# First sequence's frequency product in plain float32, its threshold subtraction on GpSimd, and another form of the MLP weights' conversion

## The chip, the cores and the metric

The kernel runs on one core of one Trainium2 chip. The metric is device time of one execution in microseconds (us), here the median of three: 1941.88 us (1940.3 to 1946.44). A core has TensorE (PE, matrix products), VectorE (DVE), ScalarE (ACT) and GpSimd (POOL), each with its own instruction queue that is worked off in order, and SyncE (SP), which here issues every DMA.

## The reference

Eight sequences of 3136 positions with 256 channels go through a frequency-domain layer and then through a block with an MLP:

```python
X = np.fft.rfft(x, axis=1)
Xr, Xi = (X.real.astype(np.float32), X.imag.astype(np.float32))
Yr = Xr @ w_r - Xi @ w_i + b_r
Yi = Xr @ w_i + Xi @ w_r + b_i
lam = 0.01
Yr = np.sign(Yr) * np.maximum(np.abs(Yr) - lam, 0.0)
Yi = np.sign(Yi) * np.maximum(np.abs(Yi) - lam, 0.0)
x = np.fft.irfft(Yr + 1j * Yi, n=x.shape[1], axis=1)
...
X = np.fft.fft(x, axis=1)
X = np.fft.fft(X, axis=2)
u = x + np.real(X).astype(np.float32)
un = (u - mean(u)) / np.sqrt(var(u) + 1e-06)
out = u + np.maximum(un @ w_ch1, 0.0) @ w_ch2
```

w_r and w_i are 256x256 in float32. The MLP weights w_ch1 (256x1024) and w_ch2 (1024x256) arrive in float64.

## The kernel before

**Split products.** Most products take operands in two parts, a high part rounded to the type float32r and a low part with the rest, also float32r. `mm3` (lines 152 to 155) then issues three matmuls: high x low, low x high, high x high. The high part is written by a copy on ACT, the low part by a subtraction, `lo_v` on VectorE (L147) or `lo_g` on GpSimd (L150).

**Stages.** The transform over 3136 = 64 x 49 positions is done in two steps by matrix products. Stage one (`p1`) makes the 64-point transforms of a sequence and stores them in DRAM (`ad`; `a0` for the first eight rows of sequence 0). `p2_f2` loads them (`af`, L415, with a table `tff`, L417) and makes the 49-point step (L431), in four quarters q of a sequence with four parts `ui` each; its result is the spectrum X of the quarter, 2 halves of 128 channels x 8 rows x (real, imaginary) x 50. `p2_w` multiplies by the complex weight, adds the bias and applies the threshold. `p2_mix` makes the channel transform of the second block's FFT2 and stores it to `md`; `p2_yt` transposes the thresholded spectrum Y (L621), `p2_g2` applies the inverse 49-point step (L648) and stores to `bd`. Then, for a pair of sequences, `p3_norm` loads `bd` (`bf`) and `md` (`mt`), makes the inverse 64-point step, adds and normalizes; `p3_tr` transposes (L731), `p3_mlp1` and `p3_mlp2` are the MLP (tiles h and o). So the MLP needs the whole of sequence 0 before it starts, and the MLP of earlier sequences hides the front stages of later ones.

**Sequence 0** has nothing to hide behind. All its stages are in plain float32 with one matmul each (`fwd_0`, `KF["cs"]`, `tif`, `yf`), except the frequency product, which uses `mm3` as for the other sequences.

**The frequency product** (L479 to 500). The complex product takes three real ones: with the sum Xs = Xr + Xi, `ks` = w_r·Xs, real part `ks` + ws·Xi, imaginary part `ks` + wd·Xr, where ws = -w_i - w_r and wd = w_i - w_r are made on VectorE at the start (L220) and split. For each quarter, each half o of the output channels and each of the three products, `prod` runs over the two halves k of the contraction. So there are 2 x 3 products of 400 columns a quarter and 24 in a sequence, each of two `mm3` (six matmuls); the prediction calls the two contraction halves of one product a pair. After the second and third, VectorE makes y = product + bias + ks (L493) and the clamp m of y to ±0.01 (L495), and Y = y - m is the threshold (L496). For sequence 0, VectorE does all of L496; for the others VectorE does half o = 0 and GpSimd o = 1. In the first quarter GpSimd also clears two elements of Y (L500 MEMSET); the transposes L621 read Y after that.

**The operands of the product** (L446 to 461). ACT copies X from PSUM to `xx`, rounds it to `Xh`, GpSimd makes `Xl`; VectorE makes the sum `xs` (L453), ACT rounds it to `Xsh`, GpSimd makes `Xsl`. For ui of 2 and 3 of sequence 0 the operands come from PSUM directly (L456 to 459): the sum is L458, and `Xl` is made on VectorE (L147). Odd quarters of sequence 0 keep the four parts in the buffers (tags) `uth`, `utl`, `bh`, `bl`, even ones in `Xh`, `Xl`, `Xsh`, `Xsl`.

**The MLP weights** (`weights`, `split_double`). They arrive as pairs of 32-bit words and are turned on the chip into high and low float32r parts, in eight tiles of 128 x 512 values. Two raw tiles of 128 x 512 words each are loaded (tags `hh`, `bf`), one tile ahead. For each half of 256 values ACT takes the absolute value of the high word (L171), VectorE keeps its sign and one exponent bit (L177) and shifts the low word (L184). On the full 512, VectorE clips (L172), shifts (L174), xors (L178), extracts the exponent (L181) and scales the low word (L186); ACT rounds the high part (L190), GpSimd subtracts it (L192) and adds the scaled low word (L193).

**What sets the order.** Each stage is a generator that yields due times; the program takes the stage with the smallest (heap at L806 to 815), with 10000 units for a sequence, a quarter of sequence 0 every 0.13 of that, and the conversion's tile j at 1.14 + 0.065 j. The framework then orders each engine's instructions by its own simulated schedule and works out the semaphores; on the chip each engine runs its list in order. `behind(key, ...)` (L262) makes a load wait in the order for the issue of an `af` load. Tiles of one tag share its buffers: a new tile waits for the last reader of the one that it replaces. In PSUM the tag `g` has four buffers for all stages up to the transposes L731.

The core of the product and the subtraction:

```python
mm3(gw, K[name][0][:, k, os_], K[name][1][:, k, os_], *r, start=k == 0, stop=k == 1)
...
va.scalar_tensor_tensor(y1, gw, bias[:, c, o:o + 1], ks, op0=ALU.add, op1=ALU.add)
m = sb.tile([128, 8, S], F32, tag="m", bufs=1, name="m")
va.tensor_scalar(m, y1, -LAM, LAM, op0=ALU.max, op1=ALU.min)
(va if b == 0 or o == 0 else gp).tensor_sub(y[:, o, :, c, :], y1, m)
```

Of the kernel before, what the change touches and what calls it, by code (L numbers as in the profile page):

```python
# [131 lines left out]
def spectral_block(ctx: ExitStack, tc: tile.TileContext, x, w_ri, b_ri, w1, w2,  # L132
# [28 lines left out]
    def split_double(name, h, l, sl, src):  # L161

        def tmp(tag, bufs, dt=I32):
            return sb.tile([128, 512], dt, tag=tag, bufs=bufs, name=f"cv_{name}_{tag}")

        halves = [(t[:, 0::2], t[:, 1::2], np.s_[:, 256 * e:256 * e + 256]) for e, t in enumerate(src)]
        tf = tmp("mt", 2, F32)
        for lo, hi, at in halves:  # L170
# [1 line left out]
        va.tensor_scalar(tf, tf, HI_MIN, HI_MAX, op0=ALU.max, op1=ALU.min)  # L172
# [3 lines left out]
        for lo, hi, at in halves:  # L176
            va.tensor_scalar(w[at], hi, -0x80000000, 0x40000000, op0=ALU.bitwise_and, op1=ALU.bitwise_or)  # L177
# [4 lines left out]
        r = tmp("mt", 2)  # L182
        for lo, hi, at in halves:
            va.tensor_scalar(r[at], lo, 8, None, op0=ALU.logical_shift_right)  # L184
# [1 line left out]
        va.scalar_tensor_tensor(rf, r, 2.0 ** -44, e.bitcast(F32), op0=ALU.mult, op1=ALU.mult)  # L186
# [22 lines left out]
    def load_consts():  # L209
# [191 lines left out]

    def p2_f2(b):


        for q in range(4):
# [57 lines left out]
    def p2_w(b):  # L463

        for q in range(4):
# [7 lines left out]
            def prod(name, o, x_, c=None):  # L473
                g = gtile("g_w")
                gw = g[:, :400].rearrange("p (a j) -> p a j", j=S)
                os_ = slice(o * 128, o * 128 + 128)
                for k in range(2):
                    r = [z[0][:, k] if len(z) == 1 else z[k] for z in x_]
                    if c is not None:  # L479
                        r = [z[:, :, c] for z in r]  # L480
                    mm3(gw, K[name][0][:, k, os_], K[name][1][:, k, os_], *r, start=k == 0, stop=k == 1)
                return gw

            for o in range(2):
# [4 lines left out]
                for c in range(2):
                    yield base + STEP * WW * (o / 2 + (c + 1) / 6)  # L490
                    gw = prod(("ws", "wd")[c], o, xs_[:2], 1 - c)
# [4 lines left out]
                    (va if b == 0 or o == 0 else gp).tensor_sub(y[:, o, :, c, :], y1, m)  # L496
# [356 lines left out]
```

## Time and profile before

| | before |
|---|---|
| median of three runs | 1941.88 us (1940.3 to 1946.44) |
| the profiled execution: span | 1937.1 us |
| instructions | 34781 |
| bytes moved by DMA | 233.03 MB, mean 120 GB/s |
| mean time of an o matmul (256 columns, L154) | 285 ns x1568 |
| mean time of an h matmul (L153) | 389 ns x832 |
| L751 on VectorE (low part of the MLP's middle layer) | 272.2 us x416 |

The span is that of the profiled execution on the core, from its first record to its last; the runs' times lie some 5 us above it, since they hold what is around it. The page gives busy time for each engine, the same in 40 slices of the span, DMA queues, the chain of work that ended last (followed back from the last instruction to what released it), and groups of instructions by line, engine and operation. In a group's row "out<-in" are the tiles written and read, "x" the count; behind the bar stand the busy time, the mean of one in ns, and the idle time just before them with what ended it. In rows of single records the first number is the start, the second the length, both in us, and square brackets hold a wait and what ended it. Tables of waits give "waiting engine, tile, line <- releaser: us, count, mean".

### The profile page before, as it was taken

The numbers are of one execution on the slowest core, as the hardware profiler recorded it, in microseconds if no ns is written. First come the engines' busy times: TensorE is split into PE (matmuls) and PEld (weight loads), VectorE is DVE, ScalarE is ACT, GpSimd is POOL, SyncE is SP. The second block draws the span as 40 slices with busy tenths as digits, with TensorE's granted clock in tenths as the row PEclk, the third lists the DMA queues.
The fourth block names the chain that finished last, engine by engine and source line by source line (L and its number), as shares of the span: only waits on it lengthen the run. The fifth ranks groups of instructions, "written<-read, shape, count | busy, mean of one in ns | idle before, by whom it ended". The sixth has DMA issues, their size and how long they took to land.

```text
span 1937.1 us, 34781 instructions
## 1 busy us (share of the span) xinstructions
PE 1841.4 (95%) x12115; PEld 1692.0 (87%) x12115; DVE 1320.5 (68%) x2847; ACT 850.6 (44%) x1896; POOL 707.5 (37%) x1087
## 2 busy tenths in 40 slices
PE   4785999999999999999999999999999999999999
PEld 2564899989999999989999999998999999998999
DVE  3974777767777667767667677766777776675543
ACT  2454545445444445444444545444544443433322
POOL 1544444344444334344333444324443332322110
PEclk7997999999999999999999999999999999999999
DMA  8766544355343545335453544435533333223210
GB/s 222 188 180 184 151 128 126 95 146 148 105 112 114 151 124 137 98 102 149 117 137 98 152 129 115 129 95 144 148 94 110 98 105 99 68 79 105 65 40 25
DMA packets 164178, 233.03 MB, mean 120 GB/s; under 512 B 27612, under 2 KB 107556, under 8 KB 164004
## 3 DMA queue, kind: packets, MB, share of 16 engines
q1 hardware_dynamic: 164004, 230.82, 42.9%
q8 instruction: 96, 1.57, 0.3%
q14 instruction: 78, 0.64, 0.1%
HBM read 127.95 MB, written 102.76 MB: 119 GB/s over the span
## 4 chain that ended last, share of the span: by engine, by line
PE 75%; DVE 5%; DMA 4%; SPq 3%; issue 1%; POOL 1%; ACT 1%; DVEq 0%; POOLq 0%; ACTq 0%
PE o L154 8%; PE o L153 8%; PE o L155 8%; PE h L153 8%; PE h L154 8%; PE h L155 8%; PE g_f L431 4%; PE g_w L153 3%; PE g_w L155 3%; PE g_w L154 3%; PE g_g L153 2%; PE g_g L154 2%; PE g_g L155 2%; PE g_ut L731 2%; PE g_yt L621 2%; DMA md<-mq 1%
## 5 line engine op out<-in xcount | busy, mean ns | idle before, releaser
L154 PE MATMUL o<-w2h,hl 128*128 128x256 f32 x1568 | 431.5, 285 | 10.9 <-DVE hl L751 10.9
L751 DVE SCALAR_TENSOR_TENSOR hl<-h,hh 128x512 fp32r<-128x512 f32 (+1 forms) x416 | 272.2, 655 | 239.8 <-ACT hh L750 238.6
L750 ACT ACTIVATE hh<-h 128x512 fp32r<-128x512 f32 (+1 forms) x416 | 238.0, 573 | 440.8 <-PE h L155 385.1
L155 PE MATMUL o<-w2h,hh 128*128 128x256 f32 x1568 | 423.9, 280 | 0.0
L153 PE MATMUL o<-w2l,hh 128*128 128x256 f32 x1568 | 397.3, 286 | 3.6 <-DVE ut L770 2.6
L153 PE MATMUL h<-utl,w1h 128*128 128x512 f32 (+1 forms) x832 | 323.5, 389 | 7.0 <-DVE hl L751 7.0
L154 PE MATMUL h<-uth,w1l 128*128 128x512 f32 (+1 forms) x832 | 318.0, 382 | 0.0
L155 PE MATMUL h<-uth,w1h 128*128 128x512 f32 (+1 forms) x832 | 316.7, 381 | 0.0
L154 PEld LDWEIGHTS o<-w2h,hl 128*128 128x128 f32 x1568 | 296.3, 189 | 18.0 <-DVE hl L751 13.6
L153 PEld LDWEIGHTS o<-w2l,hh 128*128 128x128 f32 x1568 | 285.4, 189 | 16.8 <-ACT Xsh L440 2.9
L155 PEld LDWEIGHTS o<-w2h,hh 128*128 128x128 f32 x1568 | 296.4, 189 | 3.1
L150 POOL TENSOR_TENSOR bl<-bf,bh 128x512 fp32r<-128x512 f32 x104 | 130.1, 1252 | 307.0 <-ACT bh L690 302.3
L155 PEld LDWEIGHTS h<-uth,w1h 128*128 128x128 f32 x832 | 156.8, 188 | 24.1
L153 PEld LDWEIGHTS h<-utl,w1h 128*128 128x128 f32 x832 | 157.1, 189 | 21.9 <-DVE hl L751 7.9
L431 PEld LDWEIGHTS g_f<-tff,af 98*128 98x128 f32 x1024 | 142.8, 197 | 36.3 <-issue 22.6
L431 PE MATMUL g_f<-tff,af 98*128 98x100 f32 x1024 | 149.8, 276 | 25.5 <-DMA af<-ad 12.3
L150 POOL TENSOR_TENSOR xl<-xf,xh 128x512 fp32r<-128x512 f32 (+1 forms) x75 | 98.2, 1310 | 203.2 <-ACT xh L374 197.1
L154 PEld LDWEIGHTS h<-uth,w1l 128*128 128x128 f32 x832 | 157.0, 189 | 13.0
L150 POOL TENSOR_TENSOR Xl<-xx,Xh 128x400 fp32r<-128x400 f32 (+1 forms) x96 | 107.5, 1122 | 77.0 <-ACT Xh L440 72.1
L695 DVE TENSOR_TENSOR ut<-g_g,mt 128x512 f32<-128x512 f32 x104 | 68.3, 656 | 97.2 <-PE g_g L155 72.4
L150 POOL TENSOR_TENSOR Xsl<-xs,Xsh 128x200 fp32r<-128x200 f32 x120 | 78.4, 654 | 149.3 <-ACT Xsh L440 140.6
L713 DVE TENSOR_SCALAR nm<-ut,ag,rs 128x256 f32<-128x256 f32 x196 | 88.3, 490 | 48.9 <-POOL rs L710 48.6
(155 smaller groups left out, 3790.1 us busy)
## 6 DMA issues: line engine op xcount, KB each, us to landing
bd<-bev SPq DMA_DIRECT2D x128, 196.0 KB
af<-ad SPq DMA_DIRECT2D x62, 392.0 KB
bf<-bd SPq DMA_DIRECT2D x184, 128.0 KB
out_dram<-ut SPq DMA_DIRECT2D x92, 256.0 KB
xf<-in_x SPq DMA_DIRECT2D x176, 128.0 KB
ad<-ev SPq DMA_DIRECT2D x168, 128.0 KB
md<-mq SPq DMA_DIRECT2D x112, 192.0 KB
mt<-md SPq DMA_DIRECT2D x416, 32.0 KB
```

What stands on the lines that cost most here:

```text
L150: gp.tensor_sub(out_, full, hi.bitcast(F32))
L153: te.matmul(o, lh, rl, start=start, stop=False)
L154: te.matmul(o, ll, rh, start=False, stop=False)
L155: return te.matmul(o, lh, rh, start=False, stop=stop)
L431: te.matmul(g[:, o:o + 100], afs[s][:, ui * D + k * 128:ui * D + k * 128 + 128], tfs[s][:, ui], start=True, stop=True)
L621: te.transpose(gt[:100, (v * 2 + o) * 128:(v * 2 + o + 1) * 128], y[:, o, place].rearrange("p c j -> p (c j)"), ident)
L695: va.tensor_add(ut[:, :n], g[:, :w].rearrange("p (n d) -> p n d", d=D), mt[:, :n])
L713: va.tensor_scalar(nm[:, j], ut[:, j], ag[:, j, 0:1], rs[:, j], op0=ALU.subtract, op1=ALU.mult)
L731: te.transpose(gv[:, k, j * 128:(j + 1) * 128], nm[:, j, k * 128:(k + 1) * 128], ident)
L750: sc.activation(hh[:, :w], h[:, :w], AF.Relu)
L751: va.scalar_tensor_tensor(hl[:, :w], h[:, :w], 0.0, hh[:, :w].bitcast(F32), op0=ALU.max, op1=ALU.subtract)
```

## The change

**The product.** For sequence 0 `x_tiles` now gives two plain float32 tiles, X and Xs. `p2_f2` makes them with an ACT copy from PSUM and one addition on GpSimd; `xx`, `im`, `xs` and the high and low parts are gone for that sequence. `prod` issues one plain float32 matmul for each contraction half in place of `mm3`. The unsplit w_r and ws stay in a tile with the tag `Xl` (`wrsf`), wd in one with the tag `Xsl`, for as long as sequence 0 needs them; before, they were in `hh` and `hl`.

**The threshold.** For sequence 0 all 16 subtractions Y = y - m of 128 x 400 go to GpSimd.

**The conversion.** One raw tile of 128 x 1024 words (tag `utl`, one DMA of 512 KB) takes the place of two of 128 x 512. ACT's absolute value and VectorE's and/or (L177, now L176) work on 512 values at once in place of twice 256. The clip (L172) moves to GpSimd. The shift of the low word (L184) is gone: L186 (now L182) reads the word as unsigned and multiplies by 2^-52 in place of 2^-44.

```diff
@@ split_double
-        halves = [(t[:, 0::2], t[:, 1::2], np.s_[:, 256 * e:256 * e + 256]) for e, t in enumerate(src)]
+        lo, hi = src[:, 0::2], src[:, 1::2]
         tf = tmp("mt", 2, F32)
-        for lo, hi, at in halves:
-            sc.activation(tf[at], hi.bitcast(F32), AF.Abs)
-        va.tensor_scalar(tf, tf, HI_MIN, HI_MAX, op0=ALU.max, op1=ALU.min)
+        sc.activation(tf, hi.bitcast(F32), AF.Abs)
+        gp.tensor_scalar(tf, tf, HI_MIN, HI_MAX, op0=ALU.max, op1=ALU.min)
...
-        for lo, hi, at in halves:
-            va.tensor_scalar(w[at], hi, -0x80000000, 0x40000000, op0=ALU.bitwise_and, op1=ALU.bitwise_or)
+        va.tensor_scalar(w, hi, -0x80000000, 0x40000000, op0=ALU.bitwise_and, op1=ALU.bitwise_or)
...
-        r = tmp("mt", 2)
-        for lo, hi, at in halves:
-            va.tensor_scalar(r[at], lo, 8, None, op0=ALU.logical_shift_right)
...
-        va.scalar_tensor_tensor(rf, r, 2.0 ** -44, e.bitcast(F32), op0=ALU.mult, op1=ALU.mult)
+        va.scalar_tensor_tensor(rf, lo.bitcast(U32), 2.0 ** -52, e.bitcast(F32), op0=ALU.mult, op1=ALU.mult)
@@ load_consts
-        for name, tag in (("wr", "hh"), ("ws", "hh"), ("wd", "hl")):
-            KF[name] = sb.tile([128, 2, D], F32, tag=tag, bufs=2, name=name + "f")
+        keep = sb.tile([128, 2, 2, D], F32, tag="Xl", bufs=1, name="wrsf")
+        KF["wr"], KF["ws"] = keep[:, 0], keep[:, 1]
+        KF["wd"] = sb.tile([128, 2, D], F32, tag="Xsl", bufs=1, name="wdf")
@@ x_tiles
-        if b == 0 and q % 2:
-            return [[sb.tile([128, 8] + c + [S], F32R, tag=t + z, bufs=2, name="X" + z) for k in range(2)]
-                    for t, c in (("ut", [2]), ("b", [])) for z in "hl"]
+        if b == 0:
+            if q % 2:
+                return [[sb.tile([128, 8] + c + [S], F32, tag=t + "h", bufs=2, name="X0") for k in range(2)]
+                        for t, c in (("ut", [2]), ("b", []))]
+            return [[sb.tile([128, 2, 8] + c + [S], F32, tag=t + "h", bufs=1, name="X0")]
+                    for t, c in (("X", [2]), ("Xs", []))]
@@ p2_f2
+                if b == 0:
+                    X, Xs = xq
+                    put(sc.copy, [X], gv)
+                    for x_, s_ in zip(X, Xs):
...
+                        gp.tensor_add(s_, c0, c1)
+                    continue
...
-                if ui < (3 if b else 2):
+                if ui < 3:
@@ p2_w
+                    if b == 0:
+                        te.matmul(gw, KF[name][:, k, os_], r[0], start=k == 0, stop=k == 1)
+                        continue
                     mm3(gw, K[name][0][:, k, os_], K[name][1][:, k, os_], *r, start=k == 0, stop=k == 1)
...
-                    (va if b == 0 or o == 0 else gp).tensor_sub(y[:, o, :, c, :], y1, m)
+                    (gp if b == 0 or o else va).tensor_sub(y[:, o, :, c, :], y1, m)
@@ weights
-            for e, tag in enumerate(("hh", "bf")):
-                t = sb.tile([128, 512], I32, tag=tag, bufs=2, name="raw_" + name)
-                behind(1, out=t, in_=srcs[e])
+            raw[j] = t = sb.tile([128, 1024], I32, tag="utl", bufs=2, name="raw_" + name)
+            v = t if name == "w1" else t.rearrange("p (f e) -> p f e", f=2)
+            behind(1, out=v, in_=src)
```

The change also moves instructions in the engines' lists, up to about the stage where sequence 0 ends; behind that the lists agree. Three places follow. A row is the line, the operation, the tile written and read, and the shape; "x2" stands for two such in a row.

On SP's queue, the loads around those of the second and third raw weight tile (`raw_w`), before:

```order
L266 DMA raw_w_321<-in_w 128x512
L266 DMA raw_w_323<-in_w 128x512
L417 DMA tff<-c_tf 98x400
L415 DMA af<-ad_79 98x1024 x2
L266 DMA xf<-in_x 64x512 x4
L266 DMA raw_w_424<-in_w 128x512
L266 DMA raw_w_426<-in_w 128x512
L415 DMA af<-ad_79 98x1024
L266 DMA tif<-c_ti 100x392 x2
```

and after:

```order
L263 DMA raw_w_284<-in_w 128x1024
L263 DMA tif<-c_ti 100x392
L417 DMA tff<-c_tf 98x400
L263 DMA tif<-c_ti 100x392
L415 DMA af<-ad_79 98x1024 x2
L263 DMA xf<-in_x 64x512 x4
L415 DMA af<-ad_79 98x1024
L263 DMA raw_w_352<-in_w 128x1024
L263 DMA raw_w_447<-in_w 128x1024
```

The third raw tile (raw_w_424 and raw_w_426 before, raw_w_352 after) is now issued behind the third of these `af` loads and behind both `tif` loads.

On VectorE's queue, from the conversion of that third tile on, before:

```order
L177 TENSOR_SCALAR cv_w_ut<-raw_w_424 128x256
L184 TENSOR_SCALAR cv_w_mt<-raw_w_424 128x256
L177 TENSOR_SCALAR cv_w_ut<-raw_w_426 128x256
L184 TENSOR_SCALAR cv_w_mt<-raw_w_426 128x256
L172 TENSOR_SCALAR cv_w_mt<-cv_w_mt 128x512
L174 TENSOR_SCALAR cv_w_mt<-cv_w_mt 128x512
L493 SCALAR_TENSOR_TENSOR y_369<-g_w,bias,ks 128x400
L178 TENSOR_TENSOR cv_w_ut<-cv_w_ut,cv_w_mt 128x512
L495 TENSOR_SCALAR m<-y_369 128x400
```

and after (L505 is the former L493, L507 the former L495):

```order
L176 TENSOR_SCALAR cv_w_ut<-raw_w_352 128x512
L505 SCALAR_TENSOR_TENSOR y_313<-g_w,bias,ks 128x400
L507 TENSOR_SCALAR m<-y_313 128x400
L174 TENSOR_SCALAR cv_w_mt<-cv_w_mt 128x512
L177 TENSOR_TENSOR cv_w_ut<-cv_w_ut,cv_w_mt 128x512
L505 SCALAR_TENSOR_TENSOR y_339<-g_w,bias,ks 128x400
L180 TENSOR_SCALAR cv_w_ut<-cv_w_ut 128x512
```

The first sum y of the product stands behind one operation on that raw tile in place of six.

On GpSimd's queue, between the two MEMSETs of Y in the first quarter, before:

```order
L500 MEMSET Y 128x2
L150 TENSOR_TENSOR Xl<-xs,Xh 128x100 x2
L192 TENSOR_TENSOR cv_w_ut<-cv_w_ut,w1h 128x512
L150 TENSOR_TENSOR Xl<-xs,Xh 128x100 x2
L193 TENSOR_TENSOR w1l<-cv_w_ut 128x512
L150 TENSOR_TENSOR Xl<-xx,Xh 128x2x200
L500 MEMSET Y 128x2
```

and after, with the third tile's clip ahead of them (L172 clip, L452 sum Xs, L508 subtraction Y = y - m, L512 the MEMSETs, L188 and L189 the weights' subtraction and addition):

```order
L172 TENSOR_SCALAR cv_w_mt<-cv_w_mt 128x512
L452 TENSOR_TENSOR X_263<-X_261 128x100
...
L512 MEMSET Y 128x2
L452 TENSOR_TENSOR X_264<-X_262 128x100
L508 TENSOR_TENSOR Y<-y_387,m 128x8x50
L452 TENSOR_TENSOR X_421<-X_420 128x2x100
L189 TENSOR_TENSOR w1l<-cv_w_ut 128x512
L188 TENSOR_TENSOR cv_w_ut<-cv_w_ut,w2h 128x512
L508 TENSOR_TENSOR Y<-y_404,m 128x8x50
L172 TENSOR_SCALAR cv_w_mt<-cv_w_mt 128x512 x2
L189 TENSOR_TENSOR w2l<-cv_w_ut 128x512
L512 MEMSET Y 128x2
```

Low parts `Xl` have left this stretch; sums, subtractions and clips have come. The second MEMSET now stands behind all four subtractions of the first quarter and behind five clips, counted from the one shown first.

More of the change, by code (lines that the diff above doesn't have):

```diff
@@ L13 @@
 I32 = mybir.dt.int32
+U32 = mybir.dt.uint32
 AF = mybir.ActivationFunctionType
@@ L409, in p2_f2 @@
             yield from after(("a0" if b == 0 and q == 0 else "a", b))
-            xt[b, q] = Xh, Xl, Xsh, Xsl = x_tiles(b, q)
+            xt[b, q] = xq = x_tiles(b, q)
             afs, tfs = [], []
@@ L444, in put @@
                             f(v[0], *(i[:, k] for i in ins), *v[1:])
+                if b == 0:
+                    X, Xs = xq
+                    put(sc.copy, [X], gv)
+                    for x_, s_ in zip(X, Xs):
+                        x_, s_ = (x_[:, :, us], s_[:, :, us]) if len(X) == 1 else (x_[:, us], s_[:, us])
+                        c0, c1 = (x_[:, :, :, c] if len(X) == 1 else x_[:, :, c] for c in range(2))
+                        gp.tensor_add(s_, c0, c1)
+                    continue
+                Xh, Xl, Xsh, Xsl = xq
                 xs = sb.tile([128, 2, 2, S], F32, tag="xs", bufs=2, name="xs")
-                if ui < (3 if b else 2):
+                if ui < 3:
                     xx = sb.tile([128, 2, 2, 2, S], F32, tag="xx", bufs=2, name="xx")
@@ L485, in p2_w @@
                 yield base + STEP * WW * o / 2
-                gw = prod("wr", o, xs_[2:])
+                gw = prod("wr", o, xs_[len(xs_) // 2:])
                 ks = sb.tile([128, 8, S], F32, tag="ks", bufs=2, name="ks")
@@ L490, in p2_w @@
                     yield base + STEP * WW * (o / 2 + (c + 1) / 6)
-                    gw = prod(("ws", "wd")[c], o, xs_[:2], 1 - c)
+                    gw = prod(("ws", "wd")[c], o, xs_[:len(xs_) // 2], 1 - c)
                     y1 = sb.tile([128, 8, S], F32, tag="y1", bufs=2, name="y1")
@@ L776, in weights @@
         w2v = w2.bitcast(I32).rearrange("(f p) e -> p f e", p=128)
-        todo = [("w1", np.s_[:, k, q * 512:q * 512 + 512], [w1v[:, k, (2 * q + e) * 512:(2 * q + e + 1) * 512] for e in range(2)])
+        todo = [("w1", np.s_[:, k, q * 512:q * 512 + 512], w1v[:, k, q * 1024:q * 1024 + 1024])
                 for k in range(2) for q in range(2)]
-        todo += [("w2", np.s_[:, f:f + 2, :], [w2v[:, f + e] for e in range(2)]) for f in range(0, 8, 2)]
+        todo += [("w2", np.s_[:, f:f + 2, :], w2v[:, f:f + 2]) for f in range(0, 8, 2)]
         raw = {}
         def load(j):
-            name, sl, srcs = todo[j]
-            raw[j] = []
-            for e, tag in enumerate(("hh", "bf")):
-                t = sb.tile([128, 512], I32, tag=tag, bufs=2, name="raw_" + name)
-                behind(1, out=t, in_=srcs[e])
-                raw[j].append(t)
+            name, sl, src = todo[j]
+            raw[j] = t = sb.tile([128, 1024], I32, tag="utl", bufs=2, name="raw_" + name)
+            v = t if name == "w1" else t.rearrange("p (f e) -> p f e", f=2)
+            behind(1, out=v, in_=src)
         yield T * (W_AT - W_STEP)
```

## The prediction

> **What bounds the kernel now.** I read the page first: the busy shares, then the busy tenths in 40 slices of 48.4 us each. A digit is the busy share of a slice in tenths.
>
> ```profile
> PE 1841.4 (95%) x12115; PEld 1692.0 (87%) x12115; DVE 1320.5 (68%) x2847; ACT 850.6 (44%) x1896; POOL 707.5 (37%) x1087
> PE   4785999999999999999999999999999999999999
> DVE  3974777767777667767667677766777776675543
> PE 75%; DVE 5%; DMA 4%; SPq 3%; issue 1%; POOL 1%; ACT 1%; DVEq 0%; POOLq 0%; ACTq 0%
> ```
>
> TensorE (PE) is full from the fifth slice to the end; the last line, the shares of the chain that ended last, says the same. Only in the first four slices does something else set the pace, and the third of these has VectorE (DVE) at nine tenths. All that the change touches lies there, so the second view is the table of busy time by stretches (busy us with the number of instructions, then clock, DMA share, GB/s).
>
> ```profile
> 50.50:58.00 7.50, 6.59 (x31) 5.74 (x31) 4.41 (x12) 3.29 (x8) 3.29 (x3) 0.79 0.99 242
> 58.00:81.00 23.00, 15.95 (x84) 12.29 (x84) 23.00 (x46) 10.49 (x33) 13.66 (x20) 1.00 0.77 193
> 81.00:118.00 37.00, 29.31 (x153) 22.70 (x151) 35.70 (x69) 20.75 (x58) 24.41 (x23) 0.95 0.50 142
> 118.00:145.00 27.00, 25.73 (x146) 21.67 (x144) 15.34 (x40) 14.68 (x38) 6.03 (x7) 1.00 0.76 215
> 158.00:182.00 24.00, 5.32 (x23) 4.49 (x22) 6.73 (x15) 10.91 (x24) 14.02 (x18) 0.67 0.57 159
> 225.00:1937.00 1712.00, 1685.59 (x11321) 1567.50 (x11319) 1178.60 (x2551) 746.82 (x1640) 611.75 (x969) 1.00 0.40 111
> ```
>
> Columns after the length: PE, its weight loads, DVE, ACT, POOL. From 58 to 118 us DVE is busy in 58.7 of 60 us and PE idles 14.7. From 118 to 145 PE is the bound (25.73 of 27). At 158 to 182 PE waits for the end of sequence 0's chain (threshold, channel mix, store, reload, normalization). After 225 us PE idles 26 us in 1712 and the order of all engines is the one before, so **the total moves by as much as the start moves**. The question is therefore when sequence 0's last product ends (142 us) and what its tail costs.
>
> **The change part by part.** *The product on PE.* The rows are starts and lengths of PE records.
>
> ```profile
> 91.84 0.46 PE L153 MATMUL g_w<-Xl,wsh 128*128 128x400 f32 x1
> ...
> 92.14 0.35 PE L154 MATMUL g_w<-Xh,wsl 128*128 128x400 f32 x1
> ...
> 93.08 1.02 PE L370 MATMUL g_f<-xf,fwd_f 128*128 128x512 f32 x2
> 93.93 0.25 PE L431 MATMUL g_f<-tff,af 98*128 98x100 f32 x1
> ```
>
> Six split matmuls (the two contraction halves) take 93.08 - 91.84 = 1.24 us, of which the first start-to-start step is 0.30 and each later one 0.19. The next row is a plain float32 product of 512 columns: two records, 93.93 - 93.08 = 0.85 us. For 400 columns that is 0.85 x 400/512 = 0.66, for two halves 1.33, and 1.44 with the same 0.11 lost on the first weights. So three matmuls become one and PE works **0.20 us longer** for each of the 24 pairs: +4.8 us (+2.2 without the lost 0.11).
>
> *What goes from DVE.* Counts and means of 36 to 145 us, from the groups by line and shape.
>
> ```profile
> L496 DVE TENSOR_TENSOR Y<-y,m 128x400 f32<-128x400 f32 x15 | 9.8, 654 | 0.2
> L177 DVE TENSOR_SCALAR cv_w_ut<-raw_w 128x256 int32<-128x256 int32 x16 | 8.0, 522 | 5.1 <-DMA raw_w<-in_w 5.1
> L184 DVE TENSOR_SCALAR cv_w_mt<-raw_w 128x256 int32<-128x256 int32 x16 | 7.5, 496 | 0.0
> L453 DVE TENSOR_TENSOR xs<-xx 128x200 f32<-128x200 f32 x8 | 4.6, 581 | 8.7 <-ACT xx L450 8.7
> L172 DVE TENSOR_SCALAR cv_w_mt<-cv_w_mt 128x512 f32<-128x512 f32 x8 | 4.4, 548 | 0.0
> L458 DVE TENSOR_TENSOR xs<-g_f,im 128x200 f32<-128x200 f32 x8 | 2.9, 358 | 1.3 <-POOL Xsl L150 1.2
> ```
>
> The subtractions (16, one missing here), the shifts of L184, the clips of L172, the sums of L453 and L458 and the low parts from PSUM (some 5 us, not shown) go: about 34 us. Of L177's 8.0 some 4.4 stay, by L172's mean at the same width: 38 us in all. [...]
>
> *What comes to GpSimd (POOL).*
>
> ```profile
> L150 POOL TENSOR_TENSOR Xl<-xs,Xh 128x100 fp32r<-128x100 f32 x16 | 7.4, 480 | 8.6 <-ACT Xh L444 8.5
> L192 POOL TENSOR_TENSOR cv_w_ut<-cv_w_ut,w2h 128x512 f32<-128x512 f32 x4 | 7.0, 1758 | 6.5 <-ACT w2h L190 6.5
> L150 POOL TENSOR_TENSOR Xsl<-xs,Xsh 128x200 fp32r<-128x200 f32 x8 | 5.9, 741 | 3.6 <-ACT Xsh L440 3.5
> L192 POOL TENSOR_TENSOR cv_w_ut<-cv_w_ut,w1h 128x512 f32<-128x512 f32 x4 | 5.8, 1460 | 5.8 <-ACT w1h L190 5.8
> L193 POOL TENSOR_TENSOR w2l<-cv_w_ut 128x512 fp32r<-128x512 f32 x4 | 5.7, 1420 | 1.0 <-DVE cv_w_ut L186 1.0
> L193 POOL TENSOR_TENSOR w1l<-cv_w_ut 128x512 fp32r<-128x512 f32 x4 | 5.3, 1332 | 0.8 <-DVE cv_w_ut L186 0.7
> L496 POOL TENSOR_TENSOR Y<-y,m 128x400 f32<-128x400 f32 x56 | 63.3, 1130 | 98.7 <-DVE m L495 79.0 <-PE g_g L155 14.5 <-DVE mq L563 3.4
> L709 POOL TENSOR_SCALAR vv<-vv 128x2 f32<-128x2 f32 x92 | 20.6, 223 | 7.6
> 80.11 0.10 POOL L500 MEMSET Y<- 128x2 f32 x1 [1.98 <-DVE Y L496]
> ```
>
> The two last group rows are of the whole run. It loses the low parts and keeps only the sums, but takes 16 subtractions of 1.13 us and 8 clips. A clip of 512 columns on it is in no trace. Below stands the same kind at 2 columns, 0.22 us; above the two-input operation of its width, 1.33. The two-input rows rise from 0.74 (200) to 1.33 (512), 1.9 ns a column over 0.36; with one input I halve the slope: 0.36 + 0.49 = **0.85 us**, an estimate.
>
> The work is in program order, and the order after the change shows what stands between the third clip and the second memset of Y, which PE's transposes wait for: 8 sums of 100 columns (3.84), one of 200 (0.74), 4 subtractions (4.52), 3 subtractions of the weights' high part (2 x 1.46 + 1.76 = 4.68), 3 additions (2 x 1.33 + 1.42 = 4.08), a small memset (0.1): 18.0 us, and five clips, 4.25: 22.2 us.
>
> *When that chain starts.* The clip needs ACT's absolute value of the third raw tile, and DVE's in-order queue holds the first sum y (line 493) behind that tile too.
>
> ```profile
> 56.04 0.29 DVE L177 TENSOR_SCALAR cv_w_ut<-raw_w 128x256 int32<-128x256 int32 x1 [0.54 <-DMA raw_w<-in_w]
> 57.31 0.63 DVE L493 SCALAR_TENSOR_TENSOR y<-g_w,bias,ks 128x400 f32<-128x400 f32 x1
> ...
> af<-ad SPq DMA_DIRECT2D x62, 392.0 KB
> ...
> tif<-c_ti SPq DMA_DIRECT2D x64, 153.1 KB
> ```
>
> Its second half arrives at 56.04. On SP's queue one af and two tif loads now stand ahead of it: 392 + 2 x 153.1 = 698 KB, at the 242 GB/s of 50.5 to 58 us (DMA share 0.99) 2.9 us. So it lands at 59.0 and y starts 2 us late; nothing later if the larger pieces make it up. With 0.6 us for the absolute value the chain runs from 59.6 to 81.8; before, the same memset ran at 80.11: **+1.7 us** (from -3.9, clip 0.22 and no late tile, to +4.1, clip 1.33). I count no pause on GpSimd, and its durations as they are with today's disturbance by DVE. Until there PE's 8 longer pairs and its own idle 7 us lie beside that chain. Behind a clip that waits stand sums, subtractions and memset, and behind these PE's transposes and with them all of PE.
>
> *From 81 to 145 us.* PE does 16 of the 24 pairs: +3.2 us (low +1.4). What it gets back are waits that name DVE:
>
> ```profile
> PE g_w L153 <- DVE y L493: 2.3, 1, 2.3
> ...
> PE g_mix L550 <- DVE mq L563: 1.2, 1, 1.2
> PE g_f L431 <- DVE y L493: 1.1, 1, 1.1
> PE g_g L648 <- DVE mq L563: 0.8, 1, 0.8
> ...
> PE g_f L370 <- DVE Xl L147: 0.4, 1, 0.4
> ```
>
> 5.8 us, all of it taken back, since DVE falls from 35.7 of 37 us to about half: **-2.6 us** (-4.4 to +3.2).
>
> *Tail.* The last subtraction is 1.13 in place of 0.65: **+0.5 us** (-0.5 to +1, for stores that move in their queue).
>
> *Costed at nothing.* The moved load of w_r waits for the last matmul of stage one; PE's first product follows an af load at 50.5 us, over 20 us later. The kept weights lie in tags that sequence 1 first writes at 160 us, after the last product at 142. ACT loses work and is not waited for.
>
> **Sum.** +1.7 - 2.6 + 0.5 = -0.4 us: a span of 1936.7 for 1937.1. The median of the runs, 1941.88, lies 4.8 us above that span, which I add: **1941.5 us**.
>
> **The rivals.** About 0.3% (5.8 us) is what a measurement of this kernel can tell from no change.
>
> *Within 0.3%, 0.50.* DVE's relief is paid for by GpSimd's in-order chain and PE's longer products, as summed.
>
> *Faster, 0.27.* GpSimd never binds: cheap clips, no late tile. Then PE's idle of 58 to 145 us counts, 7.05 + 7.69 + 1.27 = 16.0 us. Three quarters back (some waits name DMA) less 4.8 is -7.2: span 1929.9, **1934.7 us**. For it: PE's waits there name DVE most. Against: GpSimd is busy in 13.66 of 23 us already and its chain gets longer.
>
> [...]
>
> *Slower, 0.23.* GpSimd becomes the engine that PE waits for through the whole product stage. Place: the chain to the memset, then the other twelve subtractions. Price: clips of 1.33, memset +4.1; PE's waits only change their name, so nothing comes back, +3.2; tail +0.5: +7.8, span 1944.9, **1949.7 us**. It decides once the memset comes 2.1 us late or more with no wait won back. For it speaks that DVE and GpSimd already stretch each other:
>
> ```profile
> 85.37 1.67 DVE L496 TENSOR_TENSOR Y<-y,m 128x400 f32<-128x400 f32 x1
> 85.19 1.41 POOL L193 TENSOR_TENSOR w2l<-cv_w_ut 128x512 fp32r<-128x512 f32 x1 [0.97 <-DVE cv_w_ut L186]
> ```
>
> The subtraction took 1.67 us (mean 0.65) while GpSimd added. [...]
>
> **How the numbers follow.** The terms' ends add to -3.9 - 4.4 - 0.5 = -8.8 and +4.1 + 3.2 + 1 = +8.3, 1933 and 1950 us; the faster case lies inside and could go further, so the range is 1932 to 1951. Chances: faster 0.27, same 0.50, slower 0.23.
>
> **What would show it.** Right: the first y near 59 us, the second memset between 80 and 84, PE's idle from 81 to 145 at 3 to 5 us in place of 9, waits that name POOL, pairs of products 1.4 us apart, clips of 0.6 to 1.1. Wrong: a clip far from that, y before 57.5, PE's waits gone before 81 as well, or a tail (last product to first transposes at 182) that changes by over 2 us.

## The result: slower by 0.9%, and the profile after

The changed kernel took **1959.65 us** (median of 4 runs, 1955.55 to 1960.94), the kernel before beside it 1941.09 us: a ratio of 1.0092 (95% interval 1.0075 to 1.011); the medians differ by 18.6 us. The forecast was 1941.5 us in a range that ended at 1951. Of all executions in this document one, of the experiment f32_place below, stands apart with 4513.73 us for some 1940, and its ratio leaves it out.

The first view is the page: busy shares, and the busy tenths of PE, VectorE and GpSimd in 40 slices.

```profile
span 1958.1 us, 34567 instructions
PE 1862.2 (95%) x12067; PEld 1698.0 (87%) x12067; DVE 1301.2 (66%) x2771; ACT 840.6 (43%) x1848; POOL 725.6 (37%) x1099
PE   4785999999999999999999999999999999999999
DVE  2843777768767766767667777766777776675543
POOL 1844443344333334343333444323543332322110
```

In the second slice VectorE falls from nine tenths to eight (the forecast put that nine in the third slice, a slip of reading that no term used), and GpSimd has an eight there. PE's four slices of the start look as before, yet PE is busy 20.8 us longer in the whole: 1862.2 for 1841.4. The 24 pairs explain 4.8 of these at the forecast's 0.20 us each. Next, the busy time by stretches (length, then PE, its weight loads, VectorE, ScalarE, GpSimd, then clock, DMA share, GB/s).

```profile
58.00:81.00 23.00, 16.27 (x56) 9.41 (x55) 20.91 (x27) 7.89 (x19) 21.83 (x22) 0.85 0.67 192
81.00:118.00 37.00, 25.48 (x110) 17.34 (x110) 23.41 (x39) 14.52 (x34) 26.14 (x22) 0.88 0.43 124
118.00:145.00 27.00, 27.00 (x126) 18.29 (x125) 11.25 (x27) 13.08 (x32) 11.56 (x16) 0.97 0.62 166
```

From 58 to 81 us GpSimd is busy for 21.83 of 23 us (13.66 before): it has become the full engine. From 81 to 118 us PE idles 11.5 us, 7.7 before, and the granted clock is 0.88 in place of 0.95. What PE waited for from 58 to 118 us (line, releaser, us, count, longest):

```profile
PE g_f L431 <- DMA tff<-c_tf: 7.4, 2, 5.0
PE g_w L491 <- ACT ks L500: 4.1, 1, 4.1
PE g_f L431 <- DVE ev L375: 1.8, 1, 1.8
PE g_yt L633 <- POOL Y L512: 1.7, 1, 1.7
```

From 81 us on the waits for VectorE's y and mq are gone, as forecast (ahead of that two for y are left, of 1.2 and 0.5 us). Others stand in their place. The chain that the forecast followed is seen in GpSimd's records, with the group of its clips from 36 to 145 us:

```profile
L172 POOL TENSOR_SCALAR cv_w_mt<-cv_w_mt 128x512 f32<-128x512 f32 x8 | 16.2, 2029 | 9.1 <-ACT cv_w_mt L171 9.1
...
59.17 1.91 POOL L172 TENSOR_SCALAR cv_w_mt<-cv_w_mt 128x512 f32<-128x512 f32 x1 [3.55 <-ACT cv_w_mt L171]
...
81.92 4.07 POOL L172 TENSOR_SCALAR cv_w_mt<-cv_w_mt 128x512 f32<-128x512 f32 x2
85.96 1.46 POOL L189 TENSOR_TENSOR w2l<-cv_w_ut 128x512 fp32r<-128x512 f32 x1
87.36 0.10 POOL L512 MEMSET Y<- 128x2 f32 x1
```

A clip takes **2.03 us**, not 0.85. The chain from the third clip to the second MEMSET runs from 59.17 to 87.36: 28.2 us for 22.2. The five clips in it account for 6 us of the difference (5 x (2.03 - 0.85) = 5.9).

The 5.0 us for the table tff are another matter. The matmul that waits for it, before and after (start, length, wait):

```profile
74.82 0.66 PE L431 MATMUL g_f<-tff,af 98*128 98x100 f32 x4 [0.70 <-DMA tff<-c_tf]
```

```profile
74.86 1.15 PE L431 MATMUL g_f<-tff,af 98*128 98x100 f32 x4 [5.01 <-DMA tff<-c_tf]
```

The table is there at the same time in both. Before, PE had a part of the product and a matmul of stage one ahead of this one in its list; in the changed list they stand behind it, so PE is idle from 69.85 us.

The wait for ks comes from a clip again; its chain goes over four engines:

```profile
96.97 1.91 POOL L172 TENSOR_SCALAR cv_w_mt<-cv_w_mt 128x512 f32<-128x512 f32 x1
...
98.86 1.25 POOL L189 TENSOR_TENSOR w2l<-cv_w_ut 128x512 fp32r<-128x512 f32 x1
98.91 1.48 DVE L174 TENSOR_SCALAR cv_w_mt<-cv_w_mt 128x512 int32<-128x512 int32 x1 [2.97 <-POOL cv_w_mt L172]
...
100.43 0.91 DVE L177 TENSOR_TENSOR cv_w_ut<-cv_w_ut,cv_w_mt 128x512 int32<-128x512 int32 x1
101.38 0.62 ACT L186 CAST w2h<-cv_w_ut 128x512 fp32r<-128x512 f32 x1 [5.59 <-DVE cv_w_ut L177]
...
101.90 0.49 ACT L500 COPY ks<-g_w 128x400 f32<-128x400 f32 x1
...
102.44 0.99 PE L491 MATMUL g_w<-X,wrsf 128*128 128x400 f32 x1 [4.07 <-ACT ks L500]
```

The last clip makes VectorE wait 2.97 us. VectorE's shift then takes 1.48 us, where the same line takes 0.42 in the kernel before: GpSimd's addition began 0.05 us ahead of it, and the shift ends just behind that addition (more in the last section). ScalarE's cast waits for VectorE, the copy ks stands behind that cast in ScalarE's order, and PE waits for ks. An operation of the weights' conversion, whose result the MLP needs only after 192 us, holds four engines.

The end of the last product and the first transposes of the MLP, before and then after:

```profile
142.06 0.35 PE L155 MATMUL g_w<-Xh,wdh 128*128 128x400 f32 x1
...
182.35 0.66 PE L731 MATMUL g_ut<-ident,nm 128*128 128x128 f32 x2 [7.88 <-DVE nm L713]
```

```profile
151.49 1.51 PE L491 MATMUL g_w<-X,wdf 128*128 128x400 f32 x4
...
192.30 0.66 PE L743 MATMUL g_ut<-ident,nm 128*128 128x128 f32 x2 [7.54 <-DVE nm L725]
```

The product ends at 153.00 for 142.41, and the transposes are **10.0 us** late. The spans differ by 21.0. The other **11 us** arise behind 192 us, and from some 220 us on all engines work through the same lists as before: from the first g_ut to the end it is 1754.7 us before and 1765.8 after. The groups of the MLP's second layer, before and then after (busy us, mean ns):

```profile
L154 PE MATMUL o<-w2h,hl 128*128 128x256 f32 x1568 | 431.5, 285 | 10.9 <-DVE hl L751 10.9
L155 PE MATMUL o<-w2h,hh 128*128 128x256 f32 x1568 | 423.9, 280 | 0.0
L153 PE MATMUL o<-w2l,hh 128*128 128x256 f32 x1568 | 397.3, 286 | 3.6 <-DVE ut L770 2.6
```

```profile
L155 PE MATMUL o<-w2h,hl 128*128 128x256 f32 x1568 | 433.9, 285 | 9.3 <-DVE hl L763 9.3
L156 PE MATMUL o<-w2h,hh 128*128 128x256 f32 x1568 | 428.1, 282 | 0.0
L154 PE MATMUL o<-w2l,hh 128*128 128x256 f32 x1568 | 400.5, 288 | 4.7 <-DVE ut L782 2.8
```

The busy times of the same 4704 matmuls add up to 1262.5 us in place of 1252.7, **2 ns more each**. Since the records overlap (one lasts some 282 ns, and the next starts 116 to 119 ns after it), their difference of 9.8 us is a sign and not the time lost. A part of the 11 us is the clock: PE idles no longer in the tail (27.6 us for 29.5), but 21.5 us of it run at half clock, 11.3 before, which is worth some 5 us of PE's work (half of the 10.2 us more, an estimate). Some 6 us are left for slower matmuls. A change that touches only sequence 0 has made the MLP of all sequences slower.

### The profile page after: what moved, and what is told of

Its sections match the earlier page's. It is cut to its first block, busy times and chain, and to the rows that moved or that the text cites. A ratio compares the mean times of both kernels' runs of the same rounds, so it can differ in the third digit from the quotient of the medians.

```text
span 1958.1 us, 34567 instructions
## 1 busy us (share of the span) xinstructions
PE 1862.2 (95%) x12067; PEld 1698.0 (87%) x12067; DVE 1301.2 (66%) x2771; ACT 840.6 (43%) x1848; POOL 725.6 (37%) x1099
## 4 chain that ended last, share of the span: by engine, by line
PE 80%; DMA 7%; DVE 5%; SPq 3%; POOL 2%; issue 2%; ACT 1%; DVEq 0%; ACTq 0%; POOLq 0%
PE o L154 8%; PE o L155 8%; PE o L156 8%; PE h L154 8%; PE h L155 8%; PE h L156 8%; PE g_f L431 4%; PE g_w L154 3%; PE g_w L156 3%; PE g_w L155 3%; PE g_g L154 2%; PE g_yt L633 2%; PE g_g L156 2%; PE g_g L155 2%; PE g_ut L743 2%
## 5 line engine op out<-in xcount | busy, mean ns | idle before, releaser
L154 PEld LDWEIGHTS h<-utl,w1h 128*128 128x128 f32 x832 | 157.0, 189 | 22.2 <-DVE hl L763 7.8
L151 POOL TENSOR_TENSOR Xsl<-xs,Xsh 128x200 fp32r<-128x200 f32 x112 | 72.6, 649 | 149.1 <-ACT Xsh L440 124.9
L508 POOL TENSOR_TENSOR Y<-y,m 128x400 f32<-128x400 f32 x72 | 80.5, 1118 | 122.1 <-DVE m L507 101.8
```

The source lines that it names most:

```text
L151: gp.tensor_sub(out_, full, hi.bitcast(F32))
L154: te.matmul(o, lh, rl, start=start, stop=False)
L508: (gp if b == 0 or o else va).tensor_sub(y[:, o, :, c, :], y1, m)
```

## The experiments

One figure is used throughout: the *step*, the time from the start of an o matmul `w2h,hh` to the start of the matmul `w2l,hh` behind it, as a mean over the steps below 1.2 times their median, from 225 to 1930 us. It was worked out from the records' starts. "Tail" is the time from the first g_ut to the end of the profiled execution, "offset" the address of hh modulo 512. Addresses are those of the compiled programs. First g_ut and tail come from one execution each: the six kernels with the changed kernel's lists of instructions (changed, after_place, hh_place, hl_place, hh_up64, hh_low96) have the first g_ut between 189.3 and 194.7 us, so a few us in these columns show little by themselves.

| run | hh at (offset) | step, ns | first g_ut | tail | median | ratio to before |
|---|---|---|---|---|---|---|
| before | 91104 (480) | 116.0 | 182.3 | 1754.7 | | |
| changed | 225184 (416) | 118.6 | 192.3 | 1765.8 | 1959.65 | 1.0092 (1.0075 to 1.011) |
| clip_dve | 225184 (416) | 118.6 | 184.2 | 1765.3 | 1947.24 | 1.0029 (1.0014 to 1.0045) |
| only_f32 | 122784 (416) | 118.6 | 180.0 | 1769.6 | 1946.97 | 1.0022 (1.0009 to 1.0035) |
| only_conv | 91104 (480) | 116.0 | 188.5 | 1757.6 | 1946.35 | 1.0021 (1.0008 to 1.0034) |
| no_conv | 122784 (416) | 118.6 | 181.8 | 1765.6 | 1951.44 | 1.0050 (1.0032 to 1.0069) |
| after_place | 91104 (480) | 116.0 | 194.7 | 1755.9 | 1949.02 | 1.0036 (1.0024 to 1.0049) |
| before_place | 127584 (96) | 117.7 | 180.7 | 1767.4 | 1949.76 | 1.0044 (1.0027 to 1.0061) |
| f32_place | 91104 (480) | 115.9 | 178.8 | 1762.3 | 1941.33 | 0.9995 (0.9983 to 1.0008) |
| clip_dve_place | 91104 (480) | 116.0 | 181.4 | 1754.3 | 1937.94 | 0.9981 (0.9970 to 0.9992) |
| hh_place | 91104 (480) | 116.1 | 189.3 | 1751.5 | 1947.98 | 1.0037 (1.0022 to 1.0053) |
| hl_place | 225184 (416) | 118.6 | 189.4 | 1764.0 | 1955.81 | 1.0065 (1.0049 to 1.0081) |
| clip_half | 91104 (480) | 115.9 | 183.7 | 1755.8 | 1940.72 | 0.9990 (0.9975 to 1.0005) |
| sub_dve_place | 91104 (480) | 116.0 | 181.5 | 1755.4 | 1940.67 | 0.9998 (0.9987 to 1.0010) |
| hh_up64 | 225248 (480) | 116.1 | 190.5 | 1753.8 | 1946.55 | 1.0030 (1.0017 to 1.0043) |
| hh_low96 | 94304 (96) | 117.7 | 191.1 | 1759.7 | 1953.28 | 1.0069 (1.0054 to 1.0084) |

### The parts: clip, product, conversion

Three theories stood at the start: A, the clip on GpSimd; B, the plain float32 product with the lower clock; C, the larger raw tiles, behind which the table tff is late.

clip_dve is the changed kernel with

```diff
-        gp.tensor_scalar(tf, tf, HI_MIN, HI_MAX, op0=ALU.max, op1=ALU.min)
+        va.tensor_scalar(tf, tf, HI_MIN, HI_MAX, op0=ALU.max, op1=ALU.min)
```

> The changed kernel with one edit: the clip of the weights' conversion back on VectorE. Theory A (the clip on GpSimd: five of 2.08 us stand ahead of the second MEMSET of Y, at 87.36 us in the changed kernel, and the last one holds ScalarE's cast and behind it the copy ks, for which PE waits 4.1 us): the MEMSET comes by 80 us, the 4.1 us are gone, and at least 9 of the 18.6 us come back, 1951 us or less. Theory B (the plain float32 product, and the lower clock that its waits bring, is the cause): 1955 us or more. Theory C (the load of the table tff, for which PE waits 5.0 us at 69.85, is late because of the 512 KB raw tiles): that wait stays, and at most 5 us come back besides it, 1954 us or more.

About 12 us came back, a little more than A asked; the wait for ks is gone, while the MEMSET came at 82.35, not by 80. The 5.0 us for tff are gone too, although the raw tiles are as large as in the changed kernel, which speaks against C: this wait comes with the order of the lists, which the edit changes too. So what came back is the price of moving the clip, its time and the order together.

only_f32 is the kernel before with the parts `x_tiles`, `p2_f2`, `prod` and the place of the unsplit weights.

> The kernel before with the plain float32 product of sequence 0 alone (its operands, its sums on GpSimd and the place of the unsplit weights with it). Theory A: PE's 24 pairs cost up to 4.8 us more and VectorE loses work, so -4 to +4 us, 1937 to 1945 us. Theory B: +10 us or more, 1951 us or above.

Neither: 1946.97 lies above A's bound and below B's. Its profile made the difference: the first g_ut came at 180.0, 2.3 us *ahead* of before, and the tail took 14.9 us longer. So the product did not delay the start.

only_conv is the kernel before with `split_double` and `weights` of the change.

> The kernel before with the changed conversion alone (one raw tile of 512 KB, fewer operations on VectorE, clip on GpSimd). Theory A: the clips stand in GpSimd's order among the low parts Xl, each 2.0 us; at least +5 us, 1946 us or more. Theory B: within 3 us of before. Theory C: PE waits 4 us or more for tff near 70 us here too.

A held, but barely: 1946.35 us is just above its 1946, while the 4.3 us against the kernel before beside it are less than its 5. The start is 6.2 us late. PE waited 1.4 us for tff near 70 us, so C fell here as well. Its tail is 1757.6, near that of before.

no_conv is the changed kernel with these two functions as before.

> The changed kernel with the conversion of before (clip and shifts on VectorE, raw tiles of 256 KB): the product and the subtraction of the change remain. Theory A: within 5 us of before, 1936 to 1946 us. Theory B: 1951 us or more. Theory C: below 1947 us too, with a wait for tff of under 2 us near 70 us.

1951.44 us lies in theory B's range, but not for B's reason: the start (first g_ut 181.8) is as early as before, and the loss is all in the tail. No wait for tff exceeds 1.4 us up to 118 us. Slow tails stand in all runs that moved the unsplit weights, fast ones in the two that didn't. In the step the two groups don't overlap: 118.6 and 116.0 ns. That is theory D: hh and hl, the middle layer of the MLP, have other addresses, since before the unsplit weights were the first tiles of these tags.

### The addresses

after_place leaves every engine's list as it is in the changed kernel; the new lines stand where the unsplit weights used to be:

```diff
+        for tag in ("hh", "hh", "hl"):
+            sb.tile([128, 2, D], F32, tag=tag, bufs=2, name="place")
         keep = sb.tile([128, 2, 2, D], F32, tag="Xl", bufs=1, name="wrsf")
```

> The changed kernel, every instruction and its place in its queue as they are, with hh and hl at the addresses that they have in the kernel before (two unused tiles of hh and one of hl are created where the unsplit weights used to be). Theory D (the unsplit weights were the first tiles of hh and hl; with them gone these two, the middle layer of the MLP, lie elsewhere in SBUF, and an o matmul starts 118.6 ns after the one before it in place of 115.9): steps back to 116 ns, 2 x 1568 x 2.7 + 1568 x 0.65 = 9.5 us of PE's work gone from the part after sequence 0, its first transposes g_ut at 192 us as before, 1950 to 1952 us. If the addresses are beside the point: 1957 us or more.

The ratio falls from 1.0092 to 1.0036, some 11 us, and 1949.02 us is a little less than expected; the start stays late and the steps are back.

before_place makes the reverse in the kernel before:

```diff
-        for name, tag in (("wr", "hh"), ("ws", "hh"), ("wd", "hl")):
-            KF[name] = sb.tile([128, 2, D], F32, tag=tag, bufs=2, name=name + "f")
+        keep = sb.tile([128, 2, 2, D], F32, tag="Xl", bufs=1, name="wrsf")
+        KF["wr"], KF["ws"] = keep[:, 0], keep[:, 1]
+        KF["wd"] = sb.tile([128, 2, D], F32, tag="Xsl", bufs=1, name="wdf")
```

> The kernel before with the unsplit weights in Xl and Xsl, as the change has them, and nothing else: hh and hl move to other addresses, the product stays in three matmuls. Theory D: steps of 118 to 119 ns and +7 to +10 us, 1949 to 1952 us, with the first g_ut near 182 us. If the addresses are beside the point: 1940 to 1944 us.

+0.44% from the place of tiles that are read only before sequence 0's product, with a start 1.6 us earlier than before. PE's list is that of the kernel before (those of other engines differ a little near the start). The step is 117.7 ns, a little under the 118 expected. D holds in both directions.

f32_place and clip_dve_place put the same three lines of after_place into only_f32 and clip_dve.

> The plain float32 product alone, with hh and hl at the addresses of the kernel before. Its front was 2.3 us ahead (first g_ut at 180.0 us), so theory D: 1937 to 1941 us, below the kernel before. If PE's longer pairs and the lower clock were the price of the product: 1945 us or more, as without the addresses.

> The changed kernel with the clip on VectorE and hh and hl at the addresses of the kernel before. Both causes removed (A and D): 1947 - 9 = 1938 to 1942 us, within 0.3% of the kernel before. If one of them is not a cause: 1945 us or more.

f32_place equals the kernel before, within the interval, at 1941.33 us just above D's range. Its start is 3.5 us ahead, and its tail was 7.6 us longer in the profiled execution, with fast steps. The clock accounts for that: 29 us of this tail run at half clock, 11 of the one before, some 9 us of PE's work. clip_dve_place, the change with its two flaws removed, lies **below both kernels**: 1937.94 us, 0.9981 (0.9970 to 0.9992), a gain of some 0.2%. With A and D removed nothing of the loss is left.

hh_place and hl_place place one of the two, with ("hh", "hh") and ("mt", "hl") in the loop of after_place.

> The changed kernel with the instructions as they are and hh alone at its old address (hl lies at 102496 in place of 95200). If hh's address is what slows the o matmuls: the steps of matmuls that load hh come down from 118.6 to 116 ns and the time is about that of both in place, 1947 to 1951 us. If it is hl's: the steps stay above 117.5 ns, 1955 us or more. If each bears a part: between.

> The changed kernel with the instructions as they are and hl alone at its old address 95200 (hh stays at 225184, all weights stay where the change has them). If hl's address decides: 1947 to 1951 us and steps of 116 ns. If hh's, or that of the weights: 1955 us or more and steps of 118 to 120 ns.

With hh in its old place the whole effect is there. hl alone leaves the step at 118.6; the interval of its 1.0065 overlaps the changed kernel's, so that a small part of hl isn't excluded. In both runs other tiles move too, so the next run, in which only hh moves, is the clean test.

The last two ask what it is in the address. hh_up64 is the changed kernel with 64 unused bytes ahead of hh, which moves no other tile; hh_low96 creates hh's two buffers right behind `wdf`.

```diff
+                if (b, gi, f) == (0, 0, 0):
+                    sb.tile([128, 16], F32, tag="gap", bufs=1, name="gap")
                 hh = sb.tile([128, 512], F32R, tag="hh", bufs=2, name="hh")
```

```diff
         KF["wd"] = sb.tile([128, 2, D], F32, tag="Xsl", bufs=1, name="wdf")
+        for _ in range(2):
+            sb.tile([128, 2, D], F32, tag="hh", bufs=2, name="place")
```

> The changed kernel, every instruction and every other tile as they are, with hh alone 64 bytes higher: 225248 in place of 225184, so that it lies at 480 modulo 512 as in the kernel before (91104). If the offset within 512 bytes decides (a weight load of PE reads 512 bytes of hh a partition): steps that load hh at 116 ns, and 1947 to 1952 us. If the region of SBUF decides (hh behind the MLP weights in place of ahead of them): as the changed kernel, 1955 us or more.

> The changed kernel, every instruction as it is, with hh at 94304, 3200 bytes from its place in the kernel before and thus in the same region, but at 96 modulo 512 as in the kernel before with the moved weights (127584). If the offset within 512 bytes decides: steps of 117.5 to 118 ns and 1954 us or more. If the region decides: 116 ns and 1947 to 1952 us.

By the steps the offset decides, not the region; the time of hh_low96, 1953.28 us, lies a little under the 1954 that the offset asked for and above the region's range. 64 bytes give some 12 us: 1.0092 to 1.0030, with intervals that don't touch (1.0075 to 1.011, and 1.0017 to 1.0043). The page of hh_up64 has the three groups at before's times, in sum 1251.6 us:

```profile
L155 PE MATMUL o<-w2h,hl 128*128 128x256 f32 x1568 | 431.2, 284 | 9.5 <-DVE hl L765 9.5
L156 PE MATMUL o<-w2h,hh 128*128 128x256 f32 x1568 | 423.2, 279 | 0.0
L154 PE MATMUL o<-w2l,hh 128*128 128x256 f32 x1568 | 397.2, 286 | 4.8 <-DVE ut L784 2.7
```

Only three offsets were seen: 480 fast, 96 and 416 slow; an offset modulo 256 would fit these runs as well. hl, a stationary operand of the same size, lies at 96 in hh_place and hh_up64, and there all o steps are as fast as any, so this is no rule for every stationary operand. Which access it is, PE's weight load of hh, ScalarE's write or VectorE's read, and which offsets are good in general, stays open.

### The clip's price, and the subtraction

clip_half is after_place with one operation in the clip; the upper bound is left out.

```diff
-        gp.tensor_scalar(tf, tf, HI_MIN, HI_MAX, op0=ALU.max, op1=ALU.min)
+        gp.tensor_scalar(tf, tf, HI_MIN, None, op0=ALU.max)
```

> The changed kernel with hh and hl in place and the clip on GpSimd cut to its lower bound (one operation in place of two; the upper bound is left out). If GpSimd's price goes by operations: 1.0 to 1.2 us a clip for 2.03, the second MEMSET of Y 4 to 5 us earlier, near 83 us, and 1941 to 1946 us. If it goes by elements read and written: 2.0 us still, the MEMSET near 87 us, 1947 us or more.

The price lies between the two, and the time, 1940.72 us, just under the first range. The first clip, with GpSimd otherwise idle, in clip_half and in the changed kernel:

```profile
44.00 1.49 POOL L172 TENSOR_SCALAR cv_w_mt<-cv_w_mt 128x512 f32<-128x512 f32 x1 [4.34 <-ACT cv_w_mt L171]
```

```profile
43.75 1.91 POOL L172 TENSOR_SCALAR cv_w_mt<-cv_w_mt 128x512 f32<-128x512 f32 x1 [4.61 <-ACT cv_w_mt L171]
```

The second operation adds 0.42 us; the first, with all else, costs 1.49, more than the 1.33 of an addition of two tensors of that width. The MEMSET came at 84.5, and eight clips cheaper by 0.4 us each gave back 8 us (1949.02 to 1940.72). That is more than the 3.2 us of the clips themselves. In this run some instructions stand in another order: PE waits neither for the MEMSET nor for ks, while the wait for tff is still 5.2 us. So the clip's cost isn't told apart from the order that the framework makes of it, and the wait for tff alone was not the loss.

sub_dve_place is clip_dve_place with line 508 as before (`va if b == 0 or o == 0 else gp`).

> The changed kernel with hh and hl in place, the clip on VectorE and the threshold's subtraction back on VectorE, so that GpSimd has neither. If the subtraction on GpSimd is worth something (VectorE is busy 20.7 of 23 us from 58 to 81 us with it gone): 1940 us or more, slower than the 1937.9 with it on GpSimd. If GpSimd's chain still costs more than VectorE's: 1936 us or less. Within 1 us of 1937.9: the move of the subtraction does nothing.

1940.67 for 1937.94, in separate comparisons whose intervals (0.9987 to 1.0010, 0.9970 to 0.9992) overlap: the subtraction on GpSimd is likely worth some 3 us, not shown beyond doubt.

## Why the prediction was wrong

**The product on PE: right, at the low end.** At full clock a pair takes 1.34 to 1.45 us from start to start (the first two are 59.51 to 60.96 and 61.83 to 63.20), most of them 1.34 to 1.37. The forecast had 1.44, and 1.33 without the 0.11 lost on the first weights; so a pair costs some 0.1 us more than before, not 0.20.

```profile
59.51 1.61 PE L491 MATMUL g_w<-X,wdf 128*128 128x400 f32 x4 [1.21 <-DVE y L505]
60.96 1.03 PE L431 MATMUL g_f<-tff,af 98*128 98x100 f32 x8
61.83 1.53 PE L491 MATMUL g_w<-X,wrsf 128*128 128x400 f32 x4
63.20 1.02 PE L367 MATMUL g_f<-xf,fwd_f 128*128 128x512 f32 x2
```

**The start of GpSimd's chain: right.** The third raw tile arrived at 58.49 us (forecast 59.0), the first y came at 58.83, the chain started at 59.17 (59.6). The term's low end is a slip: a clip of 0.22 us and a tile 2.0 or 2.9 us earlier give -3.5 or -4.4 us, not -3.9; the forecast didn't rest on it.

**"A clip of 512 columns ... 0.85 us, an estimate": wrong, the first failing step.** I halved the slope because there is one input. One input was dearer than two (1.49 us in clip_half, 1.33 in the row), and the second operation cost 0.42 us extra. The upper end, 1.33, was taken for safe because it was the two-input row, and it was no bound at all. The rest of the chain was as forecast, every operation of it and 17.8 us for 18.0. Term +1.7 became +7.25 (87.36 - 80.11).

**From 81 to 145 us: -2.6 became +3.3** (the last product ends 10.6 us late, less 7.25). The 5.8 us of waits for VectorE did vanish, but 4.1 us for ks came by the last clip, and other waits with it. The granted clock, which the forecast left out, took some 5 us of PE's work (0.88 of 37 us and 0.97 of 27), 2 before (0.95 of 37). "No pause on GpSimd" was asked only of GpSimd; who waits for a clip was followed as far as the MEMSET and not through VectorE and ScalarE. The relief was smaller, too. These are groups of 36 to 145 us, before and after:

```profile
L174 DVE TENSOR_SCALAR cv_w_mt<-cv_w_mt 128x512 int32<-128x512 int32 x8 | 3.3, 416 | 0.1
```

```profile
L174 DVE TENSOR_SCALAR cv_w_mt<-cv_w_mt 128x512 int32<-128x512 int32 x8 | 8.5, 1061 | 6.6 <-POOL cv_w_mt L172 6.6
```

An unchanged instruction takes 1.06 us where it took 0.42, because it now meets GpSimd's operations (last section). From 58 to 118 us VectorE is busy 44.3 us for 58.7, and over the whole execution it lost 19.3 us, 1320.5 to 1301.2, of the 38 forecast.

**Tail: close.** +0.5 forecast, -0.6 measured: from the last product's end to the first g_ut 39.9 us before, 39.3 after.

**"The total moves by as much as the start moves": wrong, and about half of the loss.** It rested on equal lists of instructions behind 225 us. Equal lists don't have equal addresses. Neither the diff's effect on the order nor the profile of before shows an address; the move of three small tiles to other tags was the sign, and I asked only whether the new tags were free, not what the old ones would now do.

In ratios the account is: +0.92% = 0.56% for hh and hl (1.0092 less 1.0036), 0.55% for the clip (1.0036 less 0.9981), and 0.19% of gain that the rest of the change brings once both are gone. Taken in the other order it is 0.63% for the clip (1.0092 less 1.0029) and 0.48% for the addresses (1.0029 less 0.9981), and in other kernels the addresses were worth 0.27% (only_f32 to f32_place) and 0.44% (before_place). So each of the two sizes is known to some 0.1 to 0.3%. The slower rival had the right mechanism at its place, GpSimd's chain to the MEMSET, with too low a price; no rival had the address.

## What to carry to other kernels

When a change moves tiles between tags, compare the tiles' addresses as one compares the order of the instructions, and look at the mean of the hottest matmuls in stages that the change doesn't touch; 64 bytes were worth as much here as the largest part of the change. The other operations of an engine gave no upper bound here for one that had not run on it at this width (1.33 us taken for the bound, 2.03 measured): measure such an operation alone first, and follow each of its readers to the next engine before moving it behind an in-order queue. When an edit loses, run its parts alone and compare where each run is late, since two losses and a gain added up to one number here.

## What the runs showed of the hardware

**The rate of the o matmuls depended on the address of hh.** With hh at offset 480 of 512 a step took 116 ns, at 96 117.7, at 416 118.6, with the same instructions. hl at 96 cost nothing beside hh at 480.

**GpSimd's tensor_scalar** on 128x512 float32: 1.49 us with one operation (clip_half) and 1.91 with two (the changed kernel) where GpSimd had been idle; with two 2.03 in the mean.

**Operations of VectorE were held by those of GpSimd.** In the changed kernel L174 and L176 on VectorE take 0.43 us where GpSimd is idle. Nine of their sixteen records start within a sum, a subtraction or an addition on GpSimd, and all nine end 0.28 or 0.29 us behind the end of that. Of the four that start within a clip one does.

```profile
71.15 2.35 POOL L172 TENSOR_SCALAR cv_w_mt<-cv_w_mt 128x512 f32<-128x512 f32 x1
72.34 0.41 DVE L176 TENSOR_SCALAR cv_w_ut<-raw_w 128x512 int32<-128x512 int32 x1
...
73.48 1.26 POOL L188 TENSOR_TENSOR cv_w_ut<-cv_w_ut,w1h 128x512 f32<-128x512 f32 x1
73.54 1.48 DVE L174 TENSOR_SCALAR cv_w_mt<-cv_w_mt 128x512 int32<-128x512 int32 x1 [0.24 <-POOL cv_w_mt L172]
```

So these nine ended only behind GpSimd's operation. It isn't so for all: from 81 to 118 us the two engines are busy 23.41 + 26.14 = 49.6 us in 37, and 35.70 + 24.41 = 60.1 before.

**The granted clock was halved in and behind waits of PE.** These are the changed kernel's stretches around its two long waits, of 5.01 and 4.07 us (PE's busy time comes first, the granted clock is third from the end):

```profile
64.40:71.20 6.80, 4.95 (x22) 2.92 (x20) 6.73 (x9) 2.37 (x6) 6.80 (x7) 1.00 0.59 170
71.80:78.60 6.80, 3.74 (x9) 2.45 (x10) 6.46 (x9) 1.01 (x2) 6.80 (x8) 0.50 0.95 255
...
98.40:102.40 4.00, 0.00 (x0) 0.00 (x0) 3.38 (x4) 1.02 (x3) 2.72 (x4) 1.00 0.13 42
102.50:105.90 3.40, 3.40 (x5) 1.73 (x6) 0.62 (x3) 1.14 (x3) 2.42 (x2) 0.50 0.23 66
```

PE waits from 69.85 to 74.86 and gets half the clock until 78.6; it waits 4.07 us until 102.44 and then works at 0.50 for 3.4 us. So these two waits cost more than their length. Half-clock stretches also stand in the tails (6.8 us near 1342 in the changed kernel, none there before). That one too stands behind a wait, of 4.1 us for hl, with PE busy 0.24 of the 3.4 us ahead of it; behind it the h matmuls start 0.43 us apart, 0.23 before it. In the profiled executions the tails hold 11.3 us at half clock (before), 21.5 (changed) and 29 (f32_place), which is why a single profile's tail is no measure to better than a few us.
